# A gated mix of windowed attention and an MLP on one core: a new hand-written order with chosen PSUM banks, the first output chunk summed the other way round, and the maxima stored by ScalarE

## The chip, the cores and the metric

The kernel runs on one core of a Trainium2 chip. The metric is the device time in microseconds (us) of one execution; several executions are timed and the median counts, and one more execution is recorded by the hardware profiler. Engines are called PE (TensorE matmul), PEld (its weight loads), DVE (VectorE), ACT (ScalarE), POOL (GpSimd) and SP (SyncE, which here only issues DMAs). Each works through its own queue in program order.

## The reference

All tensors are float32, with S = 2048 tokens, D = 512, 32 heads of 16 and F = 1792.

```python
g = sigmoid((x * gate_w).sum(-1, keepdims=True))
q, k, v = (x @ wqkv) split into 32 heads of 16
scores = q @ k.T * 16 ** -0.5, masked to 0 <= i - j < 256
a = (softmax(scores) @ v) @ wo
y = layernorm(x)
b = gelu_tanh(y @ w1 + b1) @ w2 + b2
out = g * a + (1 - g) * b
```

## The kernel before

Every full-precision matmul is made of three single-pass ones: an operand is split into a rounded high part and the low rest (`split`, `lo_part`, L178 and L118), and high*high, high*low and low*high are summed in PSUM. The work has three stages.

**Projections.** `first_units` (L250) starts PE on 12 warm-up matmuls over a zeroed tile and then the first queries and keys, while their weights and x still arrive. The rest of the projections (`qk_unit` L288, `v_unit` L317) follow; q and k go out to DRAM, from which `load_stacks` (L330) fetches them in the layout that attention wants.

**Attention with the first MLP layer woven in.** This stage is one sequence of PE units, written out by hand as the string `ORDER` (L38), which `run` (L723) walks through. A letter `S` (`s_pair`, L339) multiplies one block of queries with its keys so that DVE can take row maxima (L357 masks, L358 reduces). `T` (`st_pair`, L394) computes the same scores transposed, with the maxima subtracted by two extra rows of the contraction; ACT takes the exponential (L405) into a p tile and POOL masks its edges (L407). `P` (`pv`, L414) multiplies the p tiles with v, one pass also summing the weights. `f` (`fill`, L694) is one of 24 steps of an `mlp1_unit` (L614), two matmuls of the first MLP layer (L626), which need nothing from attention.

Four double PSUM banks, b0 to b3, serve all of this: S, T and P take the oldest bank of the list `ring` (`two`, L103); an MLP unit takes one out for its 24 steps (L615). A bank is free again when DVE (after S) or ACT (after T, P and f) has read it.

Blocks are steps of the counter `tick` (L130); `after(k, ...)` puts work, above all DMAs on SP's queue, k steps later. `soon(n, ...)` (L138) does so by letters of `ORDER`. The maxima of four blocks go through `put_max` (L362): POOL splits them, DVE transposes them, SP stores them to DRAM (L376) and loads them back as the two extra rows (L382); `CHAIN` (L52) says how many letters after the S each of the four comes. P's sums leave for the DRAM tensor `osc` through a tile t (L425 to L437). The p tiles rotate through 7 slots (L601 to L606).

**Second MLP layer and output.** 56 items (L845), four chunks c of 512 tokens by 14 slices f, of 12 matmuls each (`mlp2`, L827, L834); `load_h` (L677) fetches the hidden values six items ahead. `attn_out` (L782) brings the attention sums: it loads the weights' sums (su) and inverts them on DVE (L790), stores them to DRAM (rd) and loads them back spread out, loads `osc` and rd in 64 KB pieces, one for each group of heads and 128 tokens (L797, L798), multiplies, splits, and runs 12 matmuls with wo for each of four token blocks (L813). It is started at item 3 in the first chunk and at f = 2 in the others. The result is scaled by the gate into a tile us (L815, L816), and after the chunk's last slice the MLP's sum is added and stored (L841, L843).

Of the kernel before, what the change touches and what calls it, by code (L numbers as in the profile page):

```python
# [19 lines left out]
S = 2048  # L20
D = 512
# [16 lines left out]
ORDER = ("TfSffSffffTSffffTSfffTfSffTfSfffTSfffSPTSTSffffTSfffTfSfPTSffSfffTSffTffTfSfTffffSTPSTSPSTfTfffTSfff"  # L38
         "TfSffTfSfffTSfffTfSffTfSfffSPSTSPTffTSffTffTffTSffSPSfffTSfffTSfffTSffTfSffSPTSfTfffTffTSffTffSfTfSf"
         "ffTSfffTfSffTffSfSPSTTPTTSPSTSPfSffTfSfffTSfffTffSfTfTffffTSffTffSffSPSffTSfffTfSffTfSfffTSfffTffSfT"  # L40
         "PSfTffTfffSTPSTSPSffTSffffTffTfSfTffSfffTSffffTSffTffSfPSTSPTfSffTfSfffTSfTfffTfSfTffSffTfSfffTSfffS"
         "PTTSPSTSPTffTSfffTfSffTfSffTSfffTfSfffTSfffTffSfSPSPfTfTSfffTfSffTSffffTSfffTfSffTfSfffTSffPTSTPSfTS"
         "ffffTSffTffSffSPSTfffTSfTfffTfSfTffffSTPSTSPfTfTSffffTffSffSPfTfSfTffSfffTSfffTfSffSPTSfTfffTffTSffT"
         "fffTfTSffffTSffTSfffTfSffSPSTSPSffTSfffTfSffTPTSfTfffSfTfSfffTfSffTfSfffSPfSTffTffSfTffSfffTSffTffSf"
         "fTPfSTPTSffTffSffSPfTfSTfffSfffTSfffTfffTSfTfffSffTSffffSPfTfTSffffTfSffTfSfffTfSfffTSfffTfSfffSPTST"
         "PTSTPSfTfSffTfSfffTSfffTfSffSfPTSffTfffSTffTffSPfTSfffTfSffTfSfffTfSffTfSfffTSfffTfffSTPTSTPSTfSffff"
         "TSfffTfSffTfSfffTSfffSPSfTffTfffSTPSTSPSffTSfffTfSfffTSfffTSffTfSfffTSfffTfSfPfSTPSfTffSfffTfSfTfffT"
         "SfTfffSffTfSffTfSfffSPTTSPSTTfffffSTPTSffTffSffTfSfffTSfffTfSffTfSffSPTSffTffTffTfTfSfSPSffTfSffTfSf"
         "ffTSfffTfSffSPTfSfTffSffTSfffTSfffSSfffTffffTffffTfTPPTTPTfTffTfTffffTfTffPfTTPTfTffTfTfffTffTfPfTTP"
         "TT")  # L50
LAG = 6
CHAIN = (6, 13, 17, 28)  # L52
# [3 lines left out]
def gated_mix_kernel(ctx, tc: tile.TileContext, xt, x2, wq0, wqk, wv, wo, xa, gw, w1, w2, b1, b2, out):  # L56
# [44 lines left out]
    ring = []  # L101

    def two():  # L103
        if not ring:
            return ps("x", (128, 2, 512))
        ring.append(ring.pop(0))
        return ps(ring[-1], (128, 2, 512))
# [142 lines left out]
    def first_units():  # L250
# [10 lines left out]
        dve.memset(idle, 0.0)  # L261
        idle = idle.bitcast(BF16)
        o = two()[:, 0]
        for _ in range(12):
            pe.matmul(o, idle[:, :128], idle[:, :512], start=True, stop=True)  # L265
# [96 lines left out]
    def put_max(p, a):  # L362
# [12 lines left out]
        def put():  # L375
            sp.dma_start(f32(view(md, [32, 4], [128, 32], [1, 32])), ms)  # L376
# [541 lines left out]
```

## Time and profile before

| what | us |
|---|---|
| median of 3 timed runs | 699.58 |
| lowest, highest of them | 697.99, 702.23 |
| the profiled execution | 699.85 |
| its span from the first to the last instruction | 698.0 |
| PE busy in it | 688.7 (99%) |
| DVE, ACT, POOL busy | 474.9, 385.1, 268.8 |

The profiled execution took 1.85 us more than its span. In a timeline row stand the start, the length, the engine, the line, the operation, the tiles it writes and reads, their size, and how many instructions are merged; in brackets the idle time before it and what ended that. Matmuls overlap in the pipe, so the length of a row is longer than its share of PE: what a matmul costs is read from one start to the next. A row of the waits has the waiting engine and line, what ended the wait, the total in us, how often, and the longest.

### The profile page before, as it was taken

How to read it: one execution, taken by the hardware profiler on the slowest of the kernel's cores; microseconds unless marked ns; L12 is line 12 of the kernel's file. 1: busy time of each engine (PE TensorE's matmuls, PEld its weight loads, DVE VectorE, ACT ScalarE, POOL GpSimd, SP SyncE). 2: the span in 40 equal slices, each digit the busy share in tenths (PEclk: the TensorE clock that was granted, in tenths of full speed). 3: DMA queues.
4: the chain of work that ended last, by engine and by line, in shares of the span. 5: the costliest groups of instructions: out<-in, count | busy, mean ns of one | idle time of the engine just before them, and what ended most of it. 6: DMA issues, size and time to landing. Idle time of an engine off the chain costs nothing.

```text
span 698.0 us, 16035 instructions
## 1 busy us (share of the span) xinstructions
PE 688.7 (99%) x5740; PEld 536.0 (77%) x5740; DVE 474.9 (68%) x971; ACT 385.1 (55%) x639; POOL 268.8 (39%) x623
## 2 busy tenths in 40 slices
PE   9999999999999999999999999999999999999997
PEld 6887777877777767777787777777777788888886
DVE  6546779966868777777687786776456835645554
ACT  6447463457686775777767768677624414123121
POOL 6900156436476564755656656559000000000000
PEclk9999999999999999999999999999999999999999
DMA  8998888786565758647776656525856443543531
GB/s 311 363 319 259 251 253 261 231 258 192 181 217 171 218 171 262 187 147 231 204 218 190 200 163 186 165 92 191 282 167 186 146 142 116 169 139 111 183 108 60
DMA packets 102678, 137.93 MB, mean 198 GB/s; under 512 B 13928, under 2 KB 53800, under 8 KB 102472
## 3 DMA queue, kind: packets, MB, share of 16 engines
q1 hardware_dynamic: 97848, 128.66, 58.7%
q10 hardware_dynamic: 4752, 8.26, 3.6%
q8 instruction: 46, 0.75, 0.4%
q14 instruction: 32, 0.26, 0.1%
HBM read 81.53 MB, written 54.30 MB: 195 GB/s over the span
## 4 chain that ended last, share of the span: by engine, by line
PE 89%; SPq 3%; DMA 3%; DVE 1%; issue 1%; ACT 1%; POOL 1%; DVEq 0%; ACTq 0%
PE ps_b L626 21%; PE ps_a L834 17%; PE ps_d L294 12%; PE ps_b L422 12%; PE ps_b L403 7%; PE ps_b L348 7%; PE ps_d L324 6%; PE ps_o L813 5%; SPq L797 1%; SPq L798 1%; DMA b2s<-in_b 1%; PE ps_d L281 1%; PE ps_x L265 1%; DMA osc<-t 1%; PE ps_x L348 1%
## 5 line engine op out<-in xcount | busy, mean ns | idle before, releaser
L626 PE MATMUL ps_b<-x,w 64*128 64x512 f32 x1344 | 212.7, 396 | 0.3 <-ACT p L405 0.2
L407 POOL TENSOR_SCALAR_AFFINE_SELECT p<-p 128x256 f32<-128x256 f32 x344 | 133.3, 415 | 102.5 <-ACT p L405 99.6
L405 ACT ACTIVATE p<-ps_b 128x768 f32<-128x768 f32 (+2 forms) x184 | 137.9, 770 | 42.5 <-PE ps_b L403 32.1
L834 PE MATMUL ps_a<-x,t 128*128 128x512 f32 x648 | 150.6, 390 | 0.8 <-DVE t L686 0.8
L358 DVE TENSOR_REDUCE mx<-ps_b 128x2 f32<-128x512 f32 x208 | 144.1, 693 | 7.1
L834 PEld LDWEIGHTS ps_a<-x,t 128*128 128x128 f32 x648 | 121.4, 188 | 27.3 <-issue 1.2
L626 PEld LDWEIGHTS ps_b<-x,w 64*128 64x128 f32 x1344 | 129.2, 186 | 11.9 <-issue 2.9
L357 DVE COPY_PREDICATED ps_b<-tri,ps_b 128x256 f32<-128x256 uint8 x208 | 88.3, 425 | 50.1 <-PE ps_b L348 34.7
L403 PE MATMUL ps_b<-qk 50*128 50x384 f32 (+5 forms) x512 | 90.3, 344 | 0.5 <-DVE mx L358 0.3
L348 PE MATMUL ps_b<-qk 62*128 62x384 f32 (+3 forms) x472 | 85.2, 346 | 1.4 <-DMA qk<-qk 1.3
L294 PE MATMUL ps_d<-x,w 128*128 128x512 f32 x360 | 84.8, 391 | 0.0
L294 PEld LDWEIGHTS ps_d<-x,w 128*128 128x128 f32 x360 | 67.3, 188 | 14.5 <-issue 0.5
L422 PE MATMUL ps_b<-p,v 128*32 128x256 f32 (+1 forms) x1376 | 74.9, 329 | 0.4 <-POOL p L407 0.4
L122 ACT ACTIVATE t<-ps_b 128x512 f32<-128x512 f32 (+1 forms) x112 | 52.0, 490 | 40.0 <-PE ps_b L422 32.8
L403 PEld LDWEIGHTS ps_b<-qk 64*128 64x128 f32 (+1 forms) x512 | 50.9, 184 | 20.7 <-issue 6.5
L407 POOL TENSOR_SCALAR_AFFINE_SELECT x<-x 128x256 f32<-128x256 f32 x136 | 52.2, 410 | 35.4 <-ACT x L405 35.1
L405 ACT ACTIVATE x<-ps_b 128x768 f32<-128x768 f32 (+2 forms) x72 | 55.0, 778 | 16.4 <-PE ps_b L403 13.6
L348 PEld LDWEIGHTS ps_b<-qk 62*128 62x128 f32 (+1 forms) x472 | 46.3, 184 | 17.9 <-ACT p L405 4.0
L422 PEld LDWEIGHTS ps_b<-p,v 128*32 128x32 f32 x1376 | 39.1, 110 | 26.5 <-ACT p L405 3.5
L119 DVE TENSOR_TENSOR t<-t,t 128x512 fp32r<-128x512 f32 x70 | 48.5, 692 | 14.6 <-ACT t L122 10.9
L122 ACT ACTIVATE t<-t 128x512 fp32r<-128x512 f32 x16 | 10.1, 632 | 81.7 <-DVE t L801 37.0
L682 ACT ACTIVATE t<-t,b1s 128x512 f32<-128x512 f32 x56 | 37.8, 715 | 25.4 <-DMA t<-hp 24.9
(87 smaller groups left out, 672.4 us busy)
## 6 DMA issues: line engine op xcount, KB each, us to landing
qk<-qk SPq DMA_DIRECT2D x112, 196.0 KB
t<-hp SPq DMA_DIRECT2D x56, 256.0 KB
hp<-t SPq DMA_DIRECT2D x52, 256.0 KB
qk<-t SPq DMA_DIRECT2D x48, 256.0 KB
osc<-t SPq DMA_DIRECT2D x31, 256.0 KB
t<-in_w SPq DMA_DIRECT2D x28, 256.0 KB
w<-w SPq DMA_DIRECT2D x28, 256.0 KB
qk<-t ACTq DMA_DIRECT2D x24, 256.0 KB
```

The source lines that it names most:

```text
L119: eng.tensor_tensor(out=lo, in0=src, in1=f32(hi), op=ALU.subtract)
L122: act.activation(dst, src, AF.Copy)
L294: pe.matmul(o, a[:, dt * 128:(dt + 1) * 128], b[:, dt * C:(dt + 1) * C], start=n == 0, stop=n == 11)
L348: pe.matmul(o[:, e, :n], qs[pr][r:k, qb * 128:qb * 128 + 128], ks[pr][r:k, t0:t0 + n], start=True, stop=True)
L357: dve.copy_predicated(o[:, :, :128], tri, o[:, :, 256:384])
L358: dve.tensor_reduce(m, o[:, :, :256], mybir.AxisListType.X, ALU.max)
L403: pe.matmul(o[:, e, :w], ks[pr][r:k, kb * 128:kb * 128 + 128], qs[pr][r:k, kb * 128:kb * 128 + w], start=True, stop=True)
L405: act.activation(pt[:, :, :w], o[:, :, :w], AF.Exp, scale=0.25)
L407: pool.affine_select(out=pt[:, :, a:a + 128], in_=pt[:, :, a:a + 128], pattern=[[0, 2], [sgn, 128]], base=b, channel_multiplier=-sgn, comp ...
L422: pe.matmul(a[32 * h:32 * h + 32, at:at + w], vs[:, kb, v:v + 32], pts[p, kb][:, h, fr:fr + w], start=n == 0, stop=n == len(parts) - 1, sk ...
L626: pe.matmul(o[:, e], w[kt // 4][r:r + 64, k, m:m + 128], y[r:r + 64, a:a + C], start=n == 0, stop=n == 23)
L834: pe.matmul(accs[c][b], x[:, b * 128:(b + 1) * 128], w, start=f == 0 and n == 0, stop=f == FT - 1 and n == 2)
```

## The change

A new `ORDER`, with 652 f in place of 647 (and 6 behind it in place of 8) and the same number of S, T and P; a string `PICK` that says for each use of a bank which place of `ring` it takes (0 the oldest; 60 times 1, once 2); an eighth p slot; P's sums go through two tiles of their own, cut from x buffers, and the t tiles of the stage become 6 in place of 9. ACT stores the maxima in this stage, 19 letters after the S in place of 17. `load_stacks` of a block is issued ahead of the work that `tick` holds for it, no longer behind it. At the start 10 warm-up matmuls in place of 12, over a zeroed tile half as large.

In the output stage `attn_out` starts at item 4 and then at f = 11 of each chunk for the next one; it loads the sums whole, one group of heads per step, in 16 large DMAs of each kind in place of 64, the inverted weights two steps behind their store, and scales ten steps after its start. In the first chunk the MLP's sum with b2 is put into us first, scaled on ACT, and the attention part is added afterwards, block by block, and stored then. wo's second half is split at step 4 and b2 loaded at step 7.

```diff
--- before.py
+++ after.py
@@ -35,21 +35,27 @@
 EPS = 1e-5
 NEG = -3.0e38
 U8 = mybir.dt.uint8
-ORDER = ("TfSffSffffTSffffTSfffTfSffTfSfffTSfffSPTSTSffffTSfffTfSfPTSffSfffTSffTffTfSfTffffSTPSTSPSTfTfffTSfff"
...
+ORDER = ("TfSfSfffffTfSfffTSfffTfSfffTSfffTfSffSPTSffTfSfffTSfffSPSTfSfffTfSfTffTffTSffTfffTSPSSTPSTfTfffTSffT"
...
+PICK = ("0000000000000000001000000000000000000001000100100000000000000000100001000100000000000001000000000000"
+        "0000000000000100010000010000000000001001001000101010001000100000000000000000001000000000100000000000"
+        "0010000000000001000010020101010000000000100101000000000000000010000001000010000000000000000100100010"
+        "1000000000100000000000000000000000000000000000000001000000000000000000010001000000000000001000000100"
+        "0000000000000000100000000000000000000000000001001100000010010000000010010000000010000010000000000010"
+        "00010000000000000000000101000100000100000000000000010000000000000000000000000000000")
 LAG = 6
-CHAIN = (6, 13, 17, 28)
+CHAIN = (6, 13, 19, 28)
 
 
 @with_exitstack
@@ -98,12 +104,15 @@
         key, bufs = banks[tag]
         return left[key].tile(list(shape), F32, name=nm("ps_" + tag), tag=tag, bufs=bufs)
 
-    ring = []
+    ring, picks = [], list(PICK)
+
+    def choose():
+        return ring.pop(int(picks.pop(0)) if picks else 0)
 
     def two():
         if not ring:
             return ps("x", (128, 2, 512))
-        ring.append(ring.pop(0))
+        ring.append(choose())
         return ps(ring[-1], (128, 2, 512))
 
     def small(tag, bufs, shape, dt=F32):
@@ -258,10 +267,10 @@
             act.dma_start(raws[:, a:b], wq0[:, a:b])
         _, hi, lo = load_x(0)
         idle = t2()
-        dve.memset(idle, 0.0)
+        dve.memset(idle[:, :256], 0.0)
         idle = idle.bitcast(BF16)
         o = two()[:, 0]
-        for _ in range(12):
+        for _ in range(10):
             pe.matmul(o, idle[:, :128], idle[:, :512], start=True, stop=True)
         loads()
         for t in range(2):
@@ -372,8 +381,8 @@
         def turn():
             dve.transpose(ms, f32(m).rearrange("p a b c d -> p (a b c d)"))
 
-        def put():
-            sp.dma_start(f32(view(md, [32, 4], [128, 32], [1, 32])), ms)
+        def put(eng=act):
+            eng.dma_start(f32(view(md, [32, 4], [128, 32], [1, 32])), ms)
 
         def rest():
             done.add(("m", p, a // 4))
@@ -383,7 +392,7 @@
 
         if spot[0] is None:
             parts()
-            after(1, lambda: (turn(), put()))
+            after(1, lambda: (turn(), put(sp)))
             after(3, rest)
         else:
             for n, fn in zip(CHAIN, (parts, turn, put, rest)):
@@ -422,7 +431,8 @@
                 pe.matmul(a[32 * h:32 * h + 32, at:at + w], vs[:, kb, v:v + 32], pts[p, kb][:, h, fr:fr + w],
                           start=n == 0, stop=n == len(parts) - 1, skip_group_check=True, tile_position=(0, 32 * h))
         if j % 2 == 0:
-            acc[p] = t2()
+            sums.append(sums.pop(0))
+            acc[p] = sums[-1]
         s = acc[p]
         o = j % 2 * 256
         if last:
@@ -592,18 +602,20 @@
     settle()
     close_pool("work")
     open_pool("work")
-    nt[0] = 9
+    nt[0] = 6
     open_psum({"b0": 1, "b1": 1}, {"b2": 1, "b3": 1})
     ring += ["b0", "b1", "b2", "b3"]
-    extra = [f32(x8())[:, :1536].rearrange("p (h n) -> p h n", h=4) for _ in range(2)]
+    extra = [f32(x8()) for _ in range(2)]
+    sums = [t[:, 1536:] for t in extra]
+    extra = [t[:, :1536].rearrange("p (h n) -> p h n", h=4) for t in extra]
     np_ = [0]
 
-    slots = [get("work", "p3", 1, (128, 3, 4, 384)), get("work", "p2", 1, (128, 2, 4, 384))]
-    slots = [slots[0][:, 0], slots[0][:, 1], extra[0], slots[0][:, 2], slots[1][:, 0], extra[1], slots[1][:, 1]]
+    low, high = (get("work", t, 1, (128, 3, 4, 384)) for t in ("pa", "pb"))
+    slots = [low[:, 0], low[:, 1], extra[0], low[:, 2], high[:, 0], extra[1], high[:, 1], high[:, 2]]
 
     def p_tile():
         np_[0] += 1
-        return slots[(np_[0] - 1) % 7]
+        return slots[(np_[0] - 1) % 8]
 
     late = []
 
@@ -612,7 +624,7 @@
     load_w1(2)
 
     def mlp1_unit(f, cp):
-        held = ring.pop(0)
+        held = choose()
         o = ps(held, (128, 2, 512))
         w = w1t[f]
         n = 0
@@ -699,12 +711,12 @@
             cur[0] = None
 
     def block(p, kb):
-        tick()
         if kb % 2 == 0:
             if kb and p + 1 < 8:
                 load_stacks(p + 1, kb * 128 - 256, 256)
             if not kb and p:
                 load_stacks(p, S - 256, 256)
+        tick()
         if p in (0, 2, 4) and kb % 2 == 0:
             double(p // 2 + 1, kb // 4, 1 - kb // 2 % 2)
         if p == 7 and kb == LAG:
@@ -738,7 +750,7 @@
             else:
                 fill()
 
-    run(ORDER + 8 * "f")
+    run(ORDER + 6 * "f")
     flush()
     for f, (gelu, _) in enumerate(early):
         gelu()
@@ -758,7 +770,7 @@
     close_pool("work")
     close_pool("ring")
     open_pool("work")
-    nt[0] = 44
+    nt[0] = 28
     waiting = {}
     for f in range(2, 4):
         waiting[0, f] = load_h(0, f)
@@ -775,8 +787,8 @@
     b2s = get("work", "b2s", 1, (128, D))
 
     after(1, gate)
-    after(1, lambda: early_wo(2, 4))
-    after(3, lambda: sp.dma_start(b2s, view(b2, [0, 128], [1, D])))
+    after(4, lambda: early_wo(2, 4))
+    after(7, lambda: sp.dma_start(b2s, view(b2, [0, 128], [1, D])))
     us = {}
 
     def attn_out(c):
@@ -785,26 +797,28 @@
             sp.dma_start(su[32 * g:32 * g + 32],
                          view(osc, [32 * S, HG], [128, 4], [1, 128], off=(g * 256 + 16) * S + c * C))
         rd = dram.tile([H, C], F32, name=nm("rd"))
+        o = get("work", "oa", 2, (128, 4, 512))
+        r = get("work", "ra", 2, (128, 4, 512))
+
+        def load_o(g):
+            sp.dma_start(o[:, g], view(osc, [32 * S, HG], [S, DH], [1, C], off=g * 256 * S + c * C))
+
+        def load_r(g):
+            sp.dma_start(r[:, g], view(rd, [C, HG], [0, DH], [1, C], off=g * HG * C))
 
         def inv():
             dve.reciprocal(su, su)
             sp.dma_start(view(rd, [128, 128], [1, 128]), su)
-            us[c] = get("work", "us", 2, (128, 4, 512))
-
-        def loads(b):
-            o, r = t2(F32, (128, 4, 128)), t2(F32, (128, 4, 128))
-            for g in range(NG):
-                sp.dma_start(o[:, g], view(osc, [32 * S, HG], [S, DH], [1, 128], off=g * 256 * S + c * C + b * 128))
-                sp.dma_start(r[:, g], view(rd, [C, HG], [0, DH], [1, 128], off=g * HG * C + b * 128))
-
-            def scale():
-                dve.tensor_tensor(out=o, in0=o, in1=r, op=ALU.mult)
-                h, l = t2(F32R, (128, 4, 128)), t2(F32R, (128, 4, 128))
-                copy(h, o)
-                lo_part(l, o, h)
-                after(1, lambda: mm(h, l))
-
-            def mm(h, l):
+            if c:
+                us[c] = get("work", "us", 2, (128, 4, 512))
+
+        def scale(b, o, r):
+            dve.tensor_tensor(out=o, in0=o, in1=r, op=ALU.mult)
+            h, l = t2(F32R, (128, 4, 128)), t2(F32R, (128, 4, 128))
+            copy(h, o)
+            lo_part(l, o, h)
+
+            def mm():
                 i = 4 * c + b
                 a = ps(f"o{b % 2}")
                 n = 0
@@ -812,15 +826,25 @@
                     for g in range(NG):
                         pe.matmul(a, x[:, g], wos[g][:, k], start=n == 0, stop=n == 11)
                         n += 1
+                if not c:
+                    dve.scalar_tensor_tensor(out=us[c][:, b], in0=a, scalar=g0[:, i:i + 1], in1=us[c][:, b],
+                                             op0=ALU.mult, op1=ALU.add)
+                    sp.dma_start(out[i], us[c][:, b])
+                    return
                 act.activation(us[c][:, b], a, AF.Copy, scale=g0[:, i:i + 1])
                 dve.scalar_tensor_tensor(out=us[c][:, b], in0=b2s, scalar=g1[:, i:i + 1], in1=us[c][:, b],
                                          op0=ALU.mult, op1=ALU.add)
 
-            after(2, scale)
-
+            after(1, mm)
+
+        load_o(0)
         after(2, inv)
+        for g in range(NG):
+            if g:
+                after(g, lambda g=g: load_o(g))
+            after(4 + g, lambda g=g: load_r(g))
         for b in range(4):
-            after(3 + b, lambda b=b: loads(b))
+            after(10 + b, lambda b=b: scale(b, *(t[:, :, b * 128:b * 128 + 128] for t in (o, r))))
 
     accs = {}
 
@@ -835,6 +859,13 @@
                           start=f == 0 and n == 0, stop=f == FT - 1 and n == 2)
             if f == FT - 1:
                 i = 4 * c + b
+                if not c:
+                    if not b:
+                        us[0] = get("work", "us", 2, (128, 4, 512))
+                    u = us[0][:, b]
+                    dve.tensor_tensor(out=u, in0=accs[c][b], in1=b2s, op=ALU.add)
+                    act.activation(u, u, AF.Copy, scale=g1[:, i:i + 1])
+                    continue
                 u = us[c][:, b]
                 for k, eng in ((0, sp), (256, act)) if i == NB - 1 else ((0, sp),):
                     cs = slice(k, k + 256 if i == NB - 1 else D)
@@ -863,8 +894,8 @@
         if item(n + 2) in waiting:
             waiting[item(n + 2)][0]()
         c, f = seq[n]
-        if f == (3 if c == 0 else 2):
-            attn_out(c)
+        if n == 4 or f == 11 and c < NCH - 1:
+            attn_out(c + (n > 4))
         mlp2(c, f)
     for key in reversed(list(left)):
         close_pool(key)
```

More of the change, by code (lines that the diff above doesn't have):

```diff
@@ L37 @@
 U8 = mybir.dt.uint8
-ORDER = ("TfSffSffffTSffffTSfffTfSffTfSfffTSfffSPTSTSffffTSfffTfSfPTSffSfffTSffTffTfSfTffffSTPSTSPSTfTfffTSfff"
[L39 to L50, printed above, removed]
```

12 lines of the change are left out of this document (added).

## Prediction

> **What bounds the kernel now.** I read the page's first lines, then PE's busy time by stretch, then the timeline of PE.
>
> ```profile
> PE 688.7 (99%) x5740; PEld 536.0 (77%) x5740; DVE 474.9 (68%) x971; ACT 385.1 (55%) x639; POOL 268.8 (39%) x623
> ```
>
> ```profile
> 6.62:145.25 138.63, 138.63 (x619) 110.47 (x617) 100.81 (x192) 70.81 (x153) 55.11 (x65) 1.00 0.89 284
> 145.25:494.54 349.29, 346.66 (x4250) 262.01 (x4249) 261.71 (x588) 250.45 (x384) 209.96 (x552) 1.00 0.62 193
> 494.54:694.10 199.56, 198.33 (x866) 161.53 (x864) 109.50 (x186) 61.66 (x98) 0.00 (x0) 1.00 0.46 146
> ```
>
> The columns are the stretch, its length, then the busy time of PE, PEld, DVE, ACT and POOL; the stretches are projections, attention (first T to first L834) and output. PE is the bound in all three: no other engine that computes is above 75% of a stretch. But a PE that is busy 346.66 of 349.29 us isn't at its peak, since a late matmul counts as long. So I price the units of attention from one start to the next, where nothing stalls:
>
> ```profile
> 308.42 0.36 PE L403 MATMUL ps_b<-qk 64*128 64x384 f32 x2
> 308.60 0.36 PE L348 MATMUL ps_b<-qk 62*128 62x384 f32 x2
> 308.78 0.85 PE L626 MATMUL ps_b<-x,w 64*128 64x512 f32 x6
> 309.47 0.34 PE L403 MATMUL ps_b<-qk 64*128 64x384 f32 x2
> ...
> 310.52 0.34 PE L348 MATMUL ps_b<-qk 48*128 48x384 f32 x2
> 310.80 0.86 PE L422 MATMUL ps_b<-p,v 128*32 128x256 f32 x16
> ...
> 312.24 0.44 PE L403 MATMUL ps_b<-qk 64*128 64x384 f32 x2
> 312.52 0.34 PE L348 MATMUL ps_b<-qk 62*128 62x384 f32 x2
> ```
>
> ```profile
> 243.39 0.79 PE ps_b L422 x16
> ...
> 467.17 2.09 PE ps_b L422 x48
> ```
>
> A T or S costs 0.18, an f (two matmuls) 0.69 / 3 = 0.23, a P 1.44 us, the half P of a pass's first block 0.79 (these two rows are of the chain of waits). The unit ahead of a P takes 0.28 in place of 0.18 and so does the one behind it: switching into and out of P costs 0.2. The stage holds 672 f (154.6 us), 492 T and S (432 of full width, 77.8; 60 of two thirds or one third, on average half of 0.18, 5.4), 56 P (80.6), 8 half ones (6.3) and 63 switches (12.6): 337.3 us. It took 349.29. So **12 us of stalls** are in attention, in pieces of 0.05 to 1.5 us, and beside fewer switches they are all that a new order can win there.
>
> The output stage has its undisturbed pace late (chain of waits) and a disturbed one early (timeline):
>
> ```profile
> 588.01 29.92 PE ps_a L834 x132
> ```
>
> ```profile
> 500.13 11.04 PE L834 MATMUL ps_a<-x,t 128*128 128x512 f32 x48
> 511.98 8.64 PE L834 MATMUL ps_a<-x,t 128*128 128x512 f32 x36 [0.81 <-DVE t L686]
> 520.71 3.06 PE L813 MATMUL ps_o<-w,t 128*128 128x512 f32 x12
> ...
> 538.32 3.02 PE L813 MATMUL ps_o<-w,t 128*128 128x512 f32 x12 [0.26 <-ACT t L122]
> ```
>
> 29.92 / 132 is 0.2267 us a matmul. From 500.13 to 538.32 stand 48 + 36 + 12 and, in the lines left out, five more groups of 12, 156 in all: 35.4 us, and it took 38.2. **2.8 us of stalls** lie there, 0.97 of them ahead of 511.98. The stage's 864 matmuls take 195.9 of its 199.56 us: 3.7 us of stalls, nearly all in the first chunk.
>
> **The change, part by part.**
>
> **Start.** The first real matmul is queued behind twelve warm-ups:
>
> ```profile
> 0.98 0.48 DVE L261 MEMSET t<- 128x512 f32 x1 [0.98 <-PEq L874]
> 1.52 5.30 PE L265 MATMUL ps_x<-t 128*128 128x512 bf16 x12 [1.52 <-DVE t L261]
> 5.23 0.51 ACT L122 ACTIVATE w<-wv 128x128 fp32r<-128x128 f32 x2 [1.73 <-DMA wv<-in_wq]
> 6.26 6.41 PE L281 MATMUL ps_d<-x,w 128*128 128x512 f32 x24
> ```
>
> Its weights are ready at 5.23 + 0.51 = 5.74. A warm-up takes 5.30 / 12 = 0.44 us; two fewer and half the memset (0.24) free PE 1.1 us sooner, and the weights then hold it to 5.75. Of the 0.9 us or less that remain, the first real matmuls give back a part, as they would run at the warm-ups' pace, half of the later one. I take -0.6, between 0 and -0.9.
>
> **Switches.** Counted in the two strings, a P stands right behind a P once before and six times after. Such a pair saves a switch (0.2) and runs in 2.09 in place of 0.79 + 1.44 (the row at 467.17): 0.3. 5 x 0.3 = -1.5 us, all on PE. Letters that leave the string come back as f behind it, so the number of f, T, S and P is the same.
>
> **The two longest stalls of attention.**
>
> ```profile
> 267.93 0.36 PE L403 MATMUL ps_b<-qk 64*128 64x384 f32 x2
> 269.61 0.44 PE L348 MATMUL ps_b<-qk 62*128 62x384 f32 x2 [1.32 <-DMA qk<-qk]
> ```
>
> ```profile
> 484.37 0.86 PE L422 MATMUL ps_b<-p,v 128*32 128x256 f32 x16
> ...
> 486.25 0.41 PE L422 MATMUL ps_b<-p,v 128*32 128x128 f32 x4 [0.38 <-POOL p L407]
> 486.59 0.44 PE L403 MATMUL ps_b<-qk 64*128 64x128 f32 x4
> ```
>
> The S at 269.61 should have come 0.18 behind the T at 267.93 and came 1.68 behind: 1.5 us lost to a late load of stacks. SP's timeline says why it was late:
>
> ```profile
> 262.61 1.28 SPq L435 DMA_DIRECT2D osc<-t  x1
> 263.98 1.79 SPq L335 DMA_DIRECT2D qk<-qk  x2
> ...
> 266.50 0.98 SPq L376 DMA_DIRECT2D md<-ms  x1
> ```
>
> The stacks stood behind the block's stores, which wait for ACT. After the change they stand ahead of them, and SP also loses the store of the maxima. I take all of it, -1.5 (0 to -1.5); next late there is the unit's bank, worth 0.2 or so elsewhere. The P at 484.37 took 2.22 in place of 1.44, waiting for POOL to mask the last p tiles. In the new string the last T and the last P are 4 f, a P and 6 f apart, 3.8 us in place of 1.8 (8 f): -0.8 (0 to -0.8).
>
> **The maxima stored by ACT.** 30 stores leave SP's queue and enter ACT's.
>
> ```profile
> L376 SPq DMA_DIRECT2D md<-ms x32: 527/594/977, 76.0 to 467.1; - x32
> ```
>
> ```profile
> L305 SPq DMA_DIRECT2D qk<-t x48: 523/566/2382, 15.2 to 144.2; - x48
> ...
> L305 ACTq DMA_DIRECT2D qk<-t x24: 524/526/702, 43.5 to 143.3; - x24
> ```
>
> ```profile
> L405 ACT ACTIVATE p<-ps_b 128x768 f32<-128x768 f32 (+2 forms) x184 | 137.9, 770 | 42.5 <-PE ps_b L403 32.1
> ```
>
> ```profile
> SPq L376 <- DVE ms L373: 12.5, 9, 4.2
> ```
>
> The one kind of store that both queues issue costs ACT about what it costs SP (medians 526 and 566 ns), so ACT gets 30 x 0.55 = 16.5 us on top of 250.45 of 349.29. Queued behind each are the exponentials, for which POOL waits, then P, and the next unit in the bank. An exponential takes 0.77 and T's come every 349 / 256 = 1.36 us: 0.59 are free between two T's, enough for one store when nothing else falls there. In the new string the T's on both sides of a store are on average 5.7 letters apart, in the old (where the store stood) 4.7; five stores have three letters or fewer, and there about 0.3 us should come through to PE. 5 x 0.3 = +1.5, between 0 and +6 (0.2 for each of the 30). ACT's waiting for the transposed maxima (SP waited up to 4.2) I put at nothing: six letters, about 1.7 us, lie between, and ACT is itself behind PE; without that cover the whole queue of exponentials would wait. SP's reload comes 9 letters behind the store in place of 11, but the store no longer queues on SP first.
>
> **Other bank waits.** Counted through both strings with the units' prices, the time from an S to the next use of its bank has the median 1.73 us in both; 50 of 236 are under 1.6 before, 35 after. From a T the median is 1.27 in both; 41 of 254 are under 1.2 before and 43 after, 6 and 11 under 1.0. `PICK`, which passes over the oldest bank 61 times, thus helps behind S and hurts a little behind T: 0, between -3 and +4, of the 9.7 us of stalls left. The eighth p slot and the other tiles cost nothing: an MLP pair needs five t tiles in about 24 us, and six are there; if that cover were short, SP's load of weights would block.
>
> **Output stage.** The stall ahead of 511.98 comes from DVE, which stood in front of the inversion of the sums with the next slice's parts queued behind it; the sums were late because SP was (the first row is DVE's timeline, the second SP's waits, the third the chain's):
>
> ```profile
> 510.01 0.95 DVE L790 RECIPROCAL su<-su 128x128 f32<-128x128 f32 x1 [6.92 <-DMA su<-osc]
> ```
>
> ```profile
> SPq L661 <- DMA osc<-t: 4.3, 1, 4.3
> ```
>
> ```profile
> 505.13 4.76 DMA su<-osc
> ```
>
> SP lost 4.3 us in front of wo's second half, whose t tile lay over a sum still being stored. With the sums outside that pool and wo three steps later SP is free, and su is asked for one step later, two steps ahead of the inversion as before. The other stalls, in front of and inside the first chunk's L813 groups, go because the scaling comes ten steps after the first load, whose 32 large DMAs replace 128. The first chunk's new sum takes the same twelve passes of DVE and ACT as before; they are hidden by the next chunk's steps (5.4 us where 12 matmuls of wo are added), else the first wo group would wait some 0.5. I take -3.0 of 3.7, between -1 and -3.5.
>
> **Sum.** -0.6 - 1.5 - 1.5 - 0.8 + 1.5 + 0 - 3.0 = -5.9 us on 699.85 (span 698.0 and 1.85 around it): 693.95, say **694.0 us**; the median of 699.58 is 0.3 below the profiled execution.
>
> **The rivals.** About 0.5% (3.5 us) is what a measurement of this kernel can tell from no change: faster is under 696.1, slower over 703.1.
>
> *The stalls of attention come back elsewhere.* The bank distances are alike, and a stall that goes lets PE run into the next late reader. For it: most stalls are short and spread. Against: the two longest have causes of their own. Without those two -3.6 remain: 696.2.
>
> *The inversion still holds DVE.* The last load of su took 4.76 us to land, and two steps of 12 matmuls are 5.4. If SP is no earlier, the output stage gives -1 only: 696.0.
>
> *ACT becomes the bound around the stores (slower).* Place: every one of the 30 stores whose next exponential comes 0.55 later while its bank is the next to be taken; the median distance of 1.27 less the exponential and about 0.3 until it starts leaves 0.2. At 0.4 us each the stores cost 12 in place of 1.5: 704.5. From (5.9 + 1.5) / 30 = 0.25 us a store on, the whole change is a loss.
>
> *Better banks.* If the new order takes half of the 9.7 us: 689.1.
>
> *Moving the queue gains nothing.* The late stacks were late by their transfer, and 1.5 us stay: 695.5. The chain's row for it shows that the transfer alone took 4.14 us:
>
> ```profile
> 265.33 4.14 DMA qk<-qk
> ```
>
> The Trainium skill's page "DMA: Bandwidth & Descriptors", section "Issuing engines are not separate DMA queues", speaks for this rival: all DMAs run on the same 16 DMA engines, so that issuing from another engine saves only the time of issuing. The rows of L305 agree that issuing costs ACT what it costs SP; whether queue or transfer made the stacks late no row settles.
>
> **How the numbers follow.** Forecast 0.40; stalls come back 0.18; inversion 0.10; ACT 0.10; better banks 0.13; queue gains nothing 0.09. The range is 689.0, where the better banks stand, to 701.0: the forecast with the stores at +6 and banks at +2 is 700.5; most of the ACT rival lies beyond. Faster: 0.34 of the forecast, 0.13, 0.06 of the last, half of the inversion's 0.10 and 0.07 of the returning stalls, 0.65. Slower: 0.08 of the ACT rival. Same: 0.27.
>
> **What would show it.** Right: the first L281 at about 5.75; no wait of L348 for qk; the stretch from the first T to the first L834 near 347; every L813 group at 2.72 us and the output stage near 196.6; ACT's idle time in attention smaller by some 16 us with PE's starts no later behind T. Wrong: an output stage still at 199 with DVE waiting for su, or an attention stage of 350 and more in which the banks behind T come free later around the new stores.

## The result, and the profile after

The changed kernel takes 692.62 us (median of 5 runs, 691.57 to 694.24) where the kernel before takes 699.58 (five runs now, 697.99 to 702.23): a ratio of 0.9893, 95% interval 0.9862 to 0.9924. The two medians alone give 0.990. The forecast was 694.0 in a range of 689.0 to 701.0. The profiled execution took 691.57 us, the shortest of the five, and its span is 689.8, 8.2 below that of before. First the page's busy times and PE's busy time by the same three stretches (projections from the first L290, attention, output):

```profile
PE 681.9 (99%) x5738; PEld 538.2 (78%) x5738; DVE 474.1 (69%) x971; ACT 385.5 (56%) x639; POOL 267.2 (39%) x623
```

```profile
5.60:144.76 139.16, 139.03 (x617) 110.09 (x618) 103.06 (x194) 71.30 (x155) 53.81 (x65) 1.00 0.89 285
144.76:488.50 343.74, 342.22 (x4250) 264.71 (x4249) 260.89 (x588) 249.87 (x384) 209.69 (x552) 1.00 0.62 195
488.50:685.95 197.45, 196.44 (x866) 162.00 (x864) 108.45 (x185) 62.60 (x98) 0.00 (x0) 1.00 0.47 149
```

Attention starts 0.5 us sooner (144.76 for 145.25), takes 343.74 for 349.29, and the output stage 197.45 for 199.56. So two thirds of the gain, 5.55 us, came from attention, of which the forecast had 2.3; the output stage gave 2.1 of the 3.0 expected. The work of the engines is the same within two warm-ups (DVE 474.1 us for 474.9, ACT 385.5 for 385.1, POOL 267.2 for 268.8); PE has fewer pauses.

PE's waits (the engine and line, what ended the wait, us, times, longest) have lost the load of stacks and the wait for POOL's masks at the end, and have new ones. The last row is an earlier P, at 203.67:

```profile
PE ps_o L827 <- ACT t L131: 1.0, 1, 1.0
PE ps_b L357 <- ACT t L131: 0.6, 1, 0.6
PE ps_b L412 <- ACT pb L414: 0.3, 1, 0.3
PE ps_b L431 <- POOL x L416: 0.2, 1, 0.2
```

The second is the first maxima store on ACT. The timeline of ACT and PE there, the sequencer's issue as ACTq:

```profile
152.93 1.05 ACTq L385 DMA_DIRECT2D md<-ms  x1
...
154.08 1.08 ACT L131 ACTIVATE t<-ps_b 128x512 f32<-128x512 f32 x2 [0.87 <-DMA md<-ms]
154.17 0.44 PE L412 MATMUL ps_b<-qk 64*128 64x384 f32 x2
...
155.22 0.44 PE L357 MATMUL ps_b<-qk 62*128 62x384 f32 x2 [0.60 <-ACT t L131]
```

The store takes 1.05 us, the two copies that free an MLP unit's bank come behind it, and the S at 155.22, which takes that bank, starts 1.05 behind the T in place of 0.28: 0.77 us lost. The other 29 stores are shorter (the group of L385) and none of them has a stall of this size behind it:

```profile
L385 ACTq DMA_DIRECT2D md<-ms x30: 510/518/1048, 152.9 to 461.6; - x30
```

The third is at the end, where the forecast saw 0.8 us to win:

```profile
478.45 0.22 PE L412 MATMUL ps_b<-qk 64*128 64x128 f32 x2
479.01 0.33 PE L412 MATMUL ps_b<-qk 64*128 64x128 f32 x2 [0.34 <-ACT pb L414]
479.50 1.20 PE L638 MATMUL ps_b<-x,w 64*128 64x512 f32 x8 [0.16 <-ACT pb L414]
```

POOL is no longer late for a P here, but the T at 478.45 is followed by one at 479.01 and that by an f at 479.50, 0.56 and 0.49 where a narrow T costs 0.06: 0.9 us, because the last narrow T's stand closer together than ACT's exponentials. The switches are as predicted: the chain has the same 2.09 for a half and a full P, and 2.74 for two full ones:

```profile
461.65 2.09 PE ps_b L431 x48
...
468.44 2.74 PE ps_b L431 x64
```

In the output stage the first chunk runs without a pause, and 156 matmuls stand on end. Then comes one gap, in front of the first wo group; that group is the first chunk's and runs among the second chunk's matmuls (PE, then DVE and ACT):

```profile
494.09 35.52 PE L858 MATMUL ps_a<-x,t 128*128 128x512 f32 x156
530.62 3.01 PE L827 MATMUL ps_o<-w,t 128*128 128x512 f32 x12 [1.00 <-ACT t L131]
```

```profile
524.88 0.95 DVE L810 RECIPROCAL su<-su 128x128 f32<-128x128 f32 x1 [6.51 <-DMA su<-osc]
```

```profile
527.48 2.56 ACT L867 ACTIVATE us<-us,g 128x512 f32<-128x512 f32 x4 [6.32 <-DVE us L866]
```

From 494.09 to 530.62 are 36.5 us for 35.4 of work. DVE stood 6.51 us in front of the inversion of the second chunk's sums, the first chunk's output sums (L866) stood behind it, ACT's scaling (L867) behind those, and the copy that the wo group needs behind that.

Where attention's stalls went can be counted unit by unit, from start to start, against the prices of the prediction (refined to 0.230 for an f, 0.174 and 0.176 for a full T and S). With these lower prices there are 14.4 us of stalls before, where the prediction had 12, and 10.4 after. Of before, 1.5 + 0.8 are the two named ones, 12.1 the rest; of after, 0.8 and 0.9 are the two shown here, 8.7 the rest. So 3.4 us came off many short waits.

### The profile page after: what moved, and what is told of

It is laid out like the page before. It is cut to its first block, busy times and chain, and to the rows that moved or that the text cites. A ratio compares the mean times of both kernels' runs of the same rounds, so it can differ in the third digit from the quotient of the medians.

```text
span 689.8 us, 15777 instructions
## 1 busy us (share of the span) xinstructions
PE 681.9 (99%) x5738; PEld 538.2 (78%) x5738; DVE 474.1 (69%) x971; ACT 385.5 (56%) x639; POOL 267.2 (39%) x623
## 4 chain that ended last, share of the span: by engine, by line
PE 86%; DMA 7%; POOL 3%; DVE 1%; ACT 1%; SPq 1%; issue 1%; ACTq 0%; DVEq 0%; POOLq 0%
PE ps_b L638 22%; PE ps_a L858 16%; PE ps_b L431 12%; PE ps_d L303 10%; PE ps_b L357 7%; PE ps_b L412 6%; PE ps_o L827 6%; PE ps_d L333 6%; DMA ra<-rd 1%; DMA hp<-t 1%; DMA t<-in_w 1%; DMA oa<-osc 1%; PE ps_x L357 1%; DMA wv<-in_wq 1%; POOL x L128 1%
## 5 line engine op out<-in xcount | busy, mean ns | idle before, releaser
L416 POOL TENSOR_SCALAR_AFFINE_SELECT pa<-pa 128x256 f32<-128x256 f32 x192 | 73.9, 412 | 68.6 <-ACT pa L414 67.9
L414 ACT ACTIVATE pa<-ps_b 128x768 f32<-128x768 f32 x96 | 76.5, 813 | 25.6 <-PE ps_b L412 18.8
L412 PE MATMUL ps_b<-qk 64*128 64x384 f32 (+5 forms) x512 | 88.8, 336 | 0.4 <-ACT pb L414 0.3
L357 PE MATMUL ps_b<-qk 62*128 62x384 f32 (+3 forms) x472 | 83.2, 345 | 0.8 <-ACT t L131 0.6
L416 POOL TENSOR_SCALAR_AFFINE_SELECT pb<-pb 128x256 f32<-128x256 f32 x160 | 62.4, 417 | 39.2 <-ACT pb L414 38.5
L414 ACT ACTIVATE pb<-ps_b 128x768 f32<-128x768 f32 (+2 forms) x96 | 65.6, 706 | 16.8 <-PE ps_b L412 12.5
L416 POOL TENSOR_SCALAR_AFFINE_SELECT x<-x 128x256 f32<-128x256 f32 x128 | 49.7, 417 | 25.8 <-ACT x L414 25.4
L357 PEld LDWEIGHTS ps_b<-qk 62*128 62x128 f32 (+1 forms) x472 | 45.4, 184 | 17.4 <-issue 3.8
L414 ACT ACTIVATE x<-ps_b 128x768 f32<-128x768 f32 x64 | 51.2, 813 | 13.0 <-PE ps_b L412 10.4
L827 PE MATMUL ps_o<-w,t 128*128 128x512 f32 x192 | 46.3, 390 | 1.0 <-ACT t L131 1.0
L333 PE MATMUL ps_d<-wv,x 128*128 128x512 f32 x192 | 46.7, 394 | 0.0
L431 PE MATMUL ps_b<-pa,v 128*32 128x256 f32 (+1 forms) x768 | 43.3, 330 | 0.2 <-POOL x L416 0.2
```

The source lines that it names most:

```text
L333: pe.matmul(o, x[:, a:a + 128], wvs[dt][:, k], start=n == 0, stop=n == 11)
L357: pe.matmul(o[:, e, :n], qs[pr][r:k, qb * 128:qb * 128 + 128], ks[pr][r:k, t0:t0 + n], start=True, stop=True)
L412: pe.matmul(o[:, e, :w], ks[pr][r:k, kb * 128:kb * 128 + 128], qs[pr][r:k, kb * 128:kb * 128 + w], start=True, stop=True)
L414: act.activation(pt[:, :, :w], o[:, :, :w], AF.Exp, scale=0.25)
L416: pool.affine_select(out=pt[:, :, a:a + 128], in_=pt[:, :, a:a + 128], pattern=[[0, 2], [sgn, 128]], base=b, channel_multiplier=-sgn, comp ...
L431: pe.matmul(a[32 * h:32 * h + 32, at:at + w], vs[:, kb, v:v + 32], pts[p, kb][:, h, fr:fr + w], start=n == 0, stop=n == len(parts) - 1, sk ...
```

## The experiments

Stages below are counted as in the expectations: the output stage up to the last matmul's start and 0.23 us, which is 0.16 less than in the rows. Ratios are against the kernel before on the same chip. Each stage time is that of one profiled execution.

**Both kernels again.** The kernel before, once; the changed one, timed.

> The kernel before, unchanged, profiled once more, because the output stage alone (3.4 us less in its profile) left the median where it was. Theory (the stalls of the first chunk in the first profile, 3.5 us over the pace of 0.2267 a matmul, are there in every execution, and the timed runs of the output stage alone scatter too far to show them): the output stage takes 199.4 within 0.5. Rival (they come and go with the DMAs): it takes 198 or less, and attention another time than 349.3 by more than 1 us.

```profile
145.27:496.63 351.36, 347.26 (x4250) 263.59 (x4249) 261.84 (x588) 250.57 (x384) 210.95 (x552) 1.00 0.63 193
496.63:694.54 197.91, 197.33 (x866) 161.70 (x864) 109.49 (x186) 61.74 (x98) 0.00 (x0) 1.00 0.47 146
```

> The changed kernel, unchanged, beside the others of this call. Theory: attention 343.7 and output 197.3 within 0.7 each, median 692 to 693, a spread of under 3 us between its runs. Rival (the spread of 7 us with the maxima stored by SP is the chip's and not the kernel's): this one spreads as far.

```profile
146.16:490.67 344.51, 342.58 (x4249) 264.48 (x4249) 261.07 (x588) 249.95 (x384) 210.57 (x552) 1.00 0.62 195
490.67:688.44 197.77, 196.61 (x866) 161.93 (x864) 108.40 (x185) 62.64 (x98) 0.00 (x0) 1.00 0.46 149
```

The rival held for the kernel before: its output stage took 197.91 by the row, against 199.56 the first time, and attention 351.36 against 349.29, with three late reloads of the maxima (1.8 us in PE's waits) that the first execution did not have. The changed kernel repeats within 0.8 in both stages, but its median here is 694.03 (6 runs, 693.09 to 697.23), ratio 0.9922 (0.9895 to 0.9949): longer and with a wider spread than the 692 to 693 and under 3 us expected. So attention's gain is 5.6 us in one pair and 6.9 in the other, and the output stage's is 2.1 in one and 0.1 in the other. Attention starts 0.5 us sooner in the first pair and 0.9 later in the second.

**The output stage alone, on the kernel before.**

```diff
 (all lines of before up to run(ORDER + 8 * "f"), then)
-    nt[0] = 44
+    nt[0] = 28
 (and everything of the changed kernel behind it)
```

> The kernel before with the output stage of the changed one alone. Theory (the output stage's gain is its own): its start, projections and attention stay at 494.5 us, the output stage falls from 199.39 to about 197.3, with the stall ahead of the first wo group of the second chunk still in it; 2.1 us in all, about 697.5. Rival (the gain needed the sums outside the t tiles and the emptier SP queue of the new attention stage): the load of wo still waits for the stored sum, DVE still waits for su, and the output stage stays above 198.5.

```profile
144.65:494.51 349.86, 346.86 (x4250) 262.04 (x4249) 261.84 (x588) 250.48 (x384) 210.08 (x552) 1.00 0.62 193
494.51:690.68 196.17, 196.17 (x866) 162.02 (x864) 108.51 (x186) 62.33 (x98) 0.00 (x0) 1.00 0.47 148
```

In this execution the output stage is at its floor, below the 197.3 expected and without the gap that the changed kernel has, so it needs nothing of the new attention stage. The median is 698.84 (12 runs, 695.74 to 701.72), ratio 1.0001 (0.9981 to 1.0021): no gain that these runs can tell. The two executions of before lose 3.4 and 1.7 us over this floor, so 2 us or more were to be expected, and the interval ends at 1.3. The profiled execution took 696.30, the second shortest of the twelve, so the others need not have this floor; how much of the difference that explains stays open.

**The banks taken oldest first.**

```diff
-PICK = ("0000000000000000001000...
+PICK = ""
```

> The changed kernel with every bank taken as the oldest of the ring; the letters stay. Theory (the picked banks are most of what attention won beyond the sum: 61 waits of some 0.05 to 0.2 us): attention takes 343.74 + 3, about 346.7, and stalls of more than 0.15 us behind S return; about 695.5. Rival (the letters do it, the picks hardly matter): below 344.7.

```profile
144.29:499.19 354.90, 348.68 (x4249) 267.18 (x4248) 262.04 (x588) 250.18 (x384) 210.00 (x552) 1.00 0.60 190
```

```profile
PE ps_b L352 <- DVE mx L362: 1.3, 4, 0.4
...
PE ps_b L633 <- DVE mx L362: 0.9, 3, 0.3
PE ps_b L407 <- DVE mx L362: 0.7, 3, 0.3
```

702.94 us (9 runs), ratio 1.0062 (1.0042 to 1.0083): slower than before. 61 choices out of 583 are worth 10.4 to 11.2 us of attention against the two executions of the changed kernel, 0.17 to 0.18 each, more than the whole change and three times the 3 us expected. The new waits shown (2.9 us) are S, f and T that wait for DVE's reduction (L362) of the S that had the oldest bank; the rest are waits for ACT and pauses too short to show as idle time. The letters are laid out for the picks, and without them are worse than the old ones.

**The old letters in the changed kernel.**

```diff
-ORDER, PICK = (the new strings)
+ORDER, PICK = (the old string), ""
-    run(ORDER + 6 * "f")
+    run(ORDER + 8 * "f")
```

> The changed kernel with the old letters and the oldest bank each time (8 f behind them); slots, tiles, ACT's stores at 19 letters, the stacks ahead and the output stage stay. Theory (letters and picks together are what attention gained, and ACT's stores cost an order that was not made for them 1 to 2 us): attention about 350; median about 698. Rival (the emptier SP queue gives the gain, whatever the letters): attention 346 or less, median under 695.

```profile
145.18:497.70 352.52, 348.10 (x4249) 264.43 (x4248) 261.55 (x588) 250.50 (x384) 210.79 (x552) 1.00 0.62 191
```

700.22 us (12 runs), ratio 1.0006 (0.9987 to 1.0026). The theory held, some 2 us above its numbers: with the old letters, the moved stacks, ACT's stores, the eighth slot and the new output stage together bring nothing that these runs can tell. About 1.7 of the 352.52 us went to a drop of the clock in this one execution, as the last section shows. Two things are left open: these letters had the store at 17 letters before and get it here at 19, and the new letters and picks were not run without the other parts.

**Each of ACT's stores twice.**

```diff
             eng.dma_start(f32(view(md, [32, 4], [128, 32], [1, 32])), ms)
+            if eng is act:
+                eng.dma_start(f32(view(md2, [32, 4], [128, 32], [1, 32])), ms)
```

> The changed kernel with each of ACT's 30 stores of the maxima issued a second time, into a DRAM tensor that nobody reads. Theory (a store costs PE about 0.05 us, for only a few of the 30 have an exponential close behind): attention 343.7 + 1.5 to 3, the second store falling outside the free time between two exponentials more often than the first; about 695. Rival (ACT has room for both): within 0.7 of 343.7. Rival (ACT is the bound around the stores): + 0.4 us each, 355 or more.

```profile
144.24:495.95 351.71, 345.99 (x4250) 262.20 (x4249) 261.49 (x588) 249.68 (x384) 210.68 (x552) 1.00 0.62 192
```

```profile
251.92 0.53 ACTq L386 DMA_DIRECT2D md<-ms  x1
252.49 0.72 ACTq L388 DMA_DIRECT2D md<-ms  x1
253.31 1.51 ACT L417 ACTIVATE pb<-ps_b 128x768 f32<-128x768 f32 x2 [2.05 <-DMA md<-ms]
```

```profile
254.17 0.45 PE L357 MATMUL ps_b<-qk 62*128 62x384 f32 x2 [1.71 <-ACT pb L417]
```

699.76 us (12 runs), ratio 1.0004 (0.9987 to 1.0021): the second store eats the whole gain. Attention is 7.2 to 8.0 us longer than in the two executions of the changed kernel, 0.24 to 0.27 a store, between the theory (0.05 to 0.1) and the rival (0.4). In the rows ACT is idle 2.05 us around a pair of stores, two exponentials wait behind them, and the S that takes the bank waits for these. So the mechanism of the prediction's slower rival is real, and the change is saved by the first store fitting. The second stores are also 30 more transfers; no run separates these from ACT's time, and the rows show only ACT's.

**The maxima stored by SP.**

```diff
-        def put(eng=act):
+        def put(eng=sp):
```

> The changed kernel with the maxima stored by SP again, still 19 letters behind the S. Theory (the stores cost ACT about 1.5 us of PE's time and spare SP's queue little, since the stacks already stand ahead of the block's stores): the attention stage takes 343.74 - 1.5, about 342.2, and the median falls to about 691. Rival (the move to ACT is what keeps SP on time): the reload of the maxima and the stacks come late again, attention takes 345.5 or more, and PE waits for a load of qk; about 694.5. Rival (nothing rides on it): 343.7 within 0.7.

```profile
144.31:488.84 344.53, 342.38 (x4250) 264.46 (x4249) 261.10 (x588) 249.54 (x384) 209.48 (x552) 1.00 0.62 195
```

694.09 us (10 runs, 691.4 to 698.8), ratio 0.992 (0.9894 to 0.9947). In the profile nothing rides on it: 344.53 against 343.74 and 344.51, so neither the gain of the theory nor the loss of its rival. But the profiled execution, 691.40, is the shortest of the ten. The 0.77 us behind the first store are gone, and PE waits 0.6 for a reload of the maxima and 0.6 for DVE instead. The spread of 7.4 us, against 2.7 and 4.1 of the changed kernel, leaves the question open here.

**The inversion one step later.** The gap in the output stage, and a version that may beat both kernels:

```diff
-        after(2, inv)
+        after(3, inv)
...
-            after(4 + g, lambda g=g: load_r(g))
+            after(5 + g, lambda g=g: load_r(g))
```

> The changed kernel with the inversion of the weights' sums three steps behind their load in place of two, and the loads of the inverted weights a step later with it. Theory (DVE waits 6.5 us for the second chunk's sums while the first chunk's output stands behind it, and that is the 1.4 us gap ahead of the first wo group): the gap goes, the output stage falls from 197.29 to about 196.1; about 691.4. Rival (that wo group is late for the new sum of the first chunk itself, twelve passes on DVE and ACT): the output stage stays at 197.0 or more, with ACT's scaling just ahead of the first wo group.

```profile
530.57 2.88 PE L827 MATMUL ps_o<-w,t 128*128 128x512 f32 x12
```

```profile
489.61:685.77 196.16, 196.16 (x866) 162.14 (x864) 108.64 (x185) 62.45 (x98) 0.00 (x0) 1.00 0.47 150
```

The gap is gone in this execution, again the shortest of its kernel, and the stage takes 196.16, its 864 matmuls at 0.2267 us plus what the last one runs on. 691.67 us (5 runs, 691.40 to 692.53), ratio 0.9895 (0.9871 to 0.9919). The same kernel, timed again, is the base of the last three, which ran on one chip with it.

> The changed kernel with the inversion three steps behind the load of the sums, once more, as the base of the three others of this call. Theory: it holds what it showed, about 1.0% under the kernel before, with no gap ahead of the first wo group, an output stage of 196.0 and attention at 344.5 within 0.7.

```profile
144.57:488.10 343.53, 342.03 (x4250) 263.59 (x4249) 260.94 (x588) 249.76 (x384) 210.63 (x552) 1.00 0.63 196
488.10:684.23 196.13, 196.13 (x866) 162.08 (x864) 108.62 (x185) 62.32 (x98) 0.00 (x0) 1.00 0.46 150
```

691.56 us (6 runs), ratio 0.9876 (0.9854 to 0.9897): the shortest of all kernels here, though its intervals overlap those of the changed kernel. That it is better rests on the stage alone, 1.3 to 1.6 us in two pairs of executions, and on the gap being absent in four of five executions with this edit. In the fifth, the store at 17 letters below, a longer wait stands in its place (the waits of PE, then the timeline of DVE):

```profile
PE ps_o L827 <- ACT t L131: 1.6, 1, 1.6
```

```profile
532.71 0.69 DVE L816 TENSOR_TENSOR oa<-oa,ra 128x512 f32<-128x512 f32 x1 [2.14 <-DMA ra<-rd]
```

There DVE waited for the inverted weights, whose loads this edit issues a step later, and the stage took 198.05. So the edit takes away one wait and leaves less room for another.

**On that base: stores by SP; the stacks behind the block's work; ACT's store at 17 letters.**

```diff
-        def put(eng=act):
+        def put(eng=sp):
```

> The base with the maxima stored by SP, 19 letters behind the S. Theory (one store fits into ACT's free time, a second does not, and on SP the store makes reloads late in some executions): its fastest runs equal the base's, its median is 1 to 3 us longer and its spread wider. Rival (no difference): medians within 0.7 and like spreads. Rival (ACT's stores cost): the median 1 us or more shorter.

```profile
PE ps_b L412 <- DMA qk<-md: 1.1, 1, 1.1
PE ps_x L357 <- DMA qk<-qk: 0.9, 1, 0.9
```

```diff
     def block(p, kb):
+        tick()
         if kb % 2 == 0:
...
-        tick()
```

> The base with the loads of the stacks behind the block's other work again, as in the kernel before. Theory (they were late behind stores that wait for ACT, and that cost the 1.5 us stall of S): a stall of 0.5 to 1.5 us ahead of an S with a load of qk as its releaser comes back, attention + 1.5. Rival (without the maxima's store SP is early enough): within 0.7 of the base, no such stall.

```profile
145.04:492.06 347.02, 343.44 (x4249) 264.74 (x4249) 260.98 (x588) 249.73 (x384) 209.66 (x552) 1.00 0.62 193
```

```profile
217.00 0.44 PE L412 MATMUL ps_b<-qk 64*128 64x384 f32 x2 [1.34 <-DMA qk<-md]
```

```diff
-CHAIN = (6, 13, 19, 28)
+CHAIN = (6, 13, 17, 28)
```

> The base with ACT's store 17 letters behind the S in place of 19. Theory (what a store costs depends on the letters around it, and 19 was laid out with the T's about a letter further apart than 17): attention + 1 to + 4 us, as 30 stores at some 0.1 us more. Rival (two letters do not matter): within 0.7.

```profile
145.02:491.45 346.43, 343.38 (x4250) 264.14 (x4249) 261.02 (x588) 249.56 (x384) 209.71 (x552) 1.00 0.62 194
```

| kernel (6 runs each) | median us | ratio (interval) | attention us | output us |
|---|---|---|---|---|
| base | 691.56 | 0.9876 (0.9854 to 0.9897) | 343.53 | 196.13 |
| stores by SP | 692.52 | 0.9891 (0.9870 to 0.9911) | 344.67 | 196.15 |
| stacks behind | 694.52 | 0.9920 (0.9897 to 0.9943) | 347.02 | 196.15 |
| store at 17 letters | 694.15 | 0.9915 (0.9891 to 0.9939) | 346.43 | 198.05 |

Stores by SP: the intervals overlap widely, though five of its six runs are longer than every run of the base, so these runs suggest that ACT's store is ahead by some 1 us, without settling it. The spread (691.29 to 693.29) is no wider than the base's (689.86 to 692.25): the wide one of the first try did not come back. PE waits for a reload of the maxima and for stacks where it waits behind ACT's first store in the base. Stacks behind: 3.5 us more attention in the profile, 3.0 in the median. The intervals touch, but all six runs (693.15 and more) are longer than every run of the base. The waits are for loads on SP's queue, the largest for the maxima's reload rather than for an S's stacks as the theory had it. Store at 17: 2.9 us more attention and 1.9 more output stage in the profile, 2.6 more in the median. Here too all six runs (692.61 and more) are longer than every run of the base, though the intervals overlap a little. That 19 suits these letters better is likely, but the output stage's wait, which the letters do not explain, is part of this profile. Profiles widen this difference, too: the base's is that of its shortest run, this one that of its second longest.

## Why the prediction was right, point by point

The number was right to 1.4 us and the direction was clear. But the largest single part of attention's gain was put at zero, other terms gave less than forecast, and that these errors nearly cancel in the sum is luck.

- *Start, -0.6*: 0.5 in the first pair, the first L290 at 5.60 (forecast 5.75). Most of it isn't the change's. In the second pair attention starts 0.9 later, and over all executions it starts at 144.96 on average with the new start (11, from 144.24 to 146.16) and at 145.06 with the old one (3): 0.1. The last section shows why the pair misleads.
- *Switches, -1.5*: counted without stalls, attention is 334.9 us before (349.29 - 14.4) and 333.3 after, -1.6. Right.
- *The late stacks, -1.5*: no wait of L357 for qk is left in the two executions of the changed kernel, and putting the stacks back cost 3.0 us in the median, with waits on SP's queue. Right, and the rival that the queue gains nothing fell: the same transfers, issued earlier, are no longer waited for. It is not the place alone, though: with the stacks ahead, PE still waits 1.2 us for them in the run with the stores by SP on the base, and 0.6 in the run of the old letters. The rule of the Trainium skill's page "DMA: Bandwidth & Descriptors", section "Issuing engines are not separate DMA queues", by which another issuing engine saves the time of issuing and no more, agrees with these runs. What helped was the place in SP's order, and SP or ACT as the maxima's issuer made a difference of some 1 us that the intervals do not settle (0.9891 against 0.9876).
- *The last P, -0.8*: POOL's wait is gone, but 0.9 of waiting for ACT's exponentials stands at the same place, so +0.1. The step that failed is "3.8 us in place of 1.8". It is the cover of the last P, which had not waited; the P at 484.37 that had is the last but one, and the p tiles that it reads are those of full T's, ahead of the two narrow ones in front of it. The new order gives it room by putting both pairs of narrow T's ahead of it. Each of these takes PE 0.06 to 0.12 us and ACT up to 0.54 for its exponential (the row of ACT at 478.36 has two in 1.08), and ACT's side was not looked at.
- *ACT's stores, +1.5*: one stall of 0.77 us, half of the forecast and inside its range; against SP's stores nothing is lost. The spread over five short gaps was wrong: it was the first store alone.
- *Other bank waits, 0 (-3 to +4)*: mis-sized, and outside its own range; the short waits fell by 3.4 us. The rival "better banks" (4.9 us) thus came true by two thirds. The count of distances compared medians and two thresholds with the picks already in, and read off that "no better and no worse". It had 50 distances behind S under 1.6 us before and 35 after, which was the better sign and was averaged away. The run without picks shows what they carry, 11.2 us.
- *Output stage, -3.0*: -2.1, and -0.1 in the second pair. The stalls that it removed were there in the one execution that was read, and half as large in the next; the output stage alone moved no median. And the rival of the inversion came true one chunk later than it was placed, 1.2 us.

Summed for the first pair: -0.5 - 1.6 - 1.5 + 0.1 + 0.8 - 3.4 - 2.1 = -8.2, the change of the span.

## What to carry to other kernels

Where the pauses of the bounding engine are many and short, price its units from start to start and count the stalls of several executions before crediting an edit with removing them; those that hang on DMAs come and go by 2 us. A hand-laid order, the choice of buffers and the place of every issue in it are one object: each alone (the letters without picks, the stores two letters sooner) lost 3 to 11 us here. One store per four blocks on ACT cost 0.8 us in all while ACT's gaps lasted, and a second one beside it half of its length each (0.25 of 0.53 us): doubling an issue shows how much room is left.

## What the runs showed of the hardware

The warm-ups' pace changes at another moment in each execution. In the traces' clock records the full clock begins 7.46 us after the first instruction in the profile of before, 6.74 in its second one, 5.17 in the output stage alone and 5.11 in the changed kernel; over all 14 executions it is 4.0 to 7.5. (The column of the granted clock reads 1.00 even before that, since no record stands there.) The start of before and of the kernel with the new output stage alone is the same code:

```profile
1.52 4.55 PE L265 MATMUL ps_x<-t 128*128 128x512 bf16 x12 [1.52 <-DVE t L261]
5.72 6.08 PE L281 MATMUL ps_d<-x,w 128*128 128x512 f32 x24
11.64 1.53 PE L294 MATMUL ps_d<-x,w 128*128 128x512 f32 x6
```

```profile
1.26 4.22 PE L274 MATMUL ps_x<-t 128*128 128x512 bf16 x10 [1.26 <-DVE t L270]
5.60 6.10 PE L290 MATMUL ps_d<-x,w 128*128 128x512 f32 x24
11.54 2.65 PE L303 MATMUL ps_d<-x,w 128*128 128x512 f32 x11
```

The first rows are of the output stage alone, the second of the changed kernel. Twelve warm-ups took 4.55 us here and 5.30 in the profile of before, and with the earlier change of pace PE is through the first 24 matmuls at 11.64, with the ten of the changed kernel at 11.54. So at nearly the same moment of change two warm-ups and half a memset are worth 0.1 us, and most of the 0.5 credited to the start was the moment at which the clock rose. That agrees with the Trainium skill, "TensorE: Matmul & The Clock Gate", section "What's actually happening", by which the clock rises after a busy window that runs free of the kernel's start, and not after a number of matmuls.

In the run of the old letters the granted clock (the third column from the end) fell for a moment in the midst of attention, right behind a pause of PE for a late reload (the stretch, then the timeline of PE):

```profile
373.00:379.00 6.00, 5.82 (x48) 4.53 (x50) 3.82 (x8) 3.34 (x6) 2.26 (x6) 0.72 0.80 249
```

```profile
373.18 0.44 PE L407 MATMUL ps_b<-qk 64*128 64x384 f32 x2 [1.72 <-DMA qk<-md]
```

6.00 x (1 - 0.72) is 1.7 us lost on top of the pause; the clock records have half the clock for 3.41 us from 374.31 on. No other of the 14 executions has such a drop inside. Whether the pause brought it on was not tried.
